# Windowed attention, forward and backward: the order of the DMA transposes on SyncE, the place of one gather, and who copies which rows

## The chip, the cores and the metric

The kernel runs on one core of a Trainium2 chip. A core has five engines, each with its own instruction queue: TensorE (PE: matmuls, with its weight loads as PEld), VectorE (DVE), ScalarE (ACT), GpSimd (POOL) and SyncE (SP), which here only starts transfers. Sixteen DMA engines move the data. The metric is device time in microseconds (us), as the median of several runs; a profiled execution gives a trace of every instruction and every DMA packet.

## What is computed

The input x is an image of 256 × 256 positions with C = 384 channels in bfloat16, cut into 1024 windows of 8 × 8 = 64 tokens. Each window goes through one attention head of width 384 and an output projection. Wanted are the output and the gradients of x, wqkv and wo for a given grad_out.

```python
def _fwd_reference(x, wqkv, wo):
    ...
    qkv = xw @ wqkv
    q, k, v = (qkv[..., :C].copy(), qkv[..., C:2 * C].copy(), qkv[..., 2 * C:].copy())
    scale = C ** (-0.5)
    p = _softmax(jnp.einsum('bqc,bkc->bqk', q, k) * scale, axis=-1)
    o = jnp.einsum('bqk,bkc->bqc', p, v) @ wo
    ...
    _out, _vjp = jax.vjp(_f, x, wqkv, wo)
    _grads = _vjp(grad_out)
```

## The kernel before

**Algebra.** q and k are never formed. With A = scale·Wq·Wkᵀ and B = Wv·Wo, both made once at the start, the scores are x·A·xᵀ and the output is P·(x·B). Per token the kernel forms y (x times A) and z (the output gradient times Bᵀ), both with channels on the partitions, and u = x·B and v = x·Aᵀ with tokens on the partitions. Weight gradients are gathered in two sums, GF_acc, and turned into the gradients of wqkv and wo after the last window.

**Tiles.** Eight windows (a column of 64 rows and 8 columns) are a *quad*: QUAD = 4 tiles of 128 tokens, two windows each. There are 128 quads. For each, x and grad_out are loaded with tokens on the partitions (xq, dq), and both are needed transposed as well (xT, dT); the transposes are done by the DMA engines, started from SP, except for the first quads, which TensorE transposes. Two more DMA transposes per quad follow: `to_tokens` (L174) turns z and y, gathered in zy, into tok (24 blocks of 128 × 128), and `turn` (L244) turns the probabilities and their gradients, stacked in ps, into PS (4 blocks). xT and dT have 12 blocks each.

**Order.** The kernel writes the order of every engine's instructions out by hand (`manual_schedule`); each engine executes its own in the order of the program. The outer loop (L453) runs a step for each i. In step i three quads are in work: a = i+1 gets its projections z and y (`project`, L154), b = i its scores, softmax and u and v (`scores`, `soft`, `uv`), and c = i-1 its attention products and outputs (`attention`, `attend`). The step also loads quad i+3 (`load`, L122: two of the four x tiles from SP, all gradient tiles from POOL; the other two x tiles from ACT, `load_rest`). Ahead of step i, `load_turn` (L134) starts dT and xT of quad i+2.

So SP issues, in each round: dT and xT of quad i+2 (L139), PS of quad i (L246), two x tiles of quad i+3 (L127), tok of quad i+1 (L176). An instruction that has to wait holds up all that stand behind it on the same engine.

**Who uses what.** xT of quad i+2 is read from the y projections of step i+1 on, dT by the z projections of that step. tok and PS of quad i are read by the attention of step i+1. The buffers: xT has 3, dT 2, zy 2, tok 3, PS 2, x 10, dq 6. A z gather of quad i+2 therefore overwrites the zy that tok of quad i was read from, and xT of quad i+2 needs x of quad i+2, loaded in step i-1.

**Copies.** All matmul results go through eight PSUM banks (`ring`), each freed when VectorE or ScalarE has copied it out. The table EV (L388) says who copies: a letter for each tile, D for VectorE, A for ScalarE. "d" is the gradient of x: tile t's copy is of a bank that holds halves of two tiles; the first covers 64 rows, and a fifth copy covers the last 64.

**The gathers.** `gather` (L168) copies z (kind 0) and y (kind 1) out of the interleaved yz into zy, 128 × 1536 values each, on VectorE. The z gather comes ahead of the y projections, the y gather inside the attention of the step: `attention` yields after every tile, and L380 to L384 put the gather behind the first one:

```python
        slots = attention(c) if c is not None else iter(())
        next(slots, None)
        A(gather, 1)
        A(to_tokens)
        for rest in slots:
            pass
```

Of the kernel before, what the change touches and what calls it, by code (L numbers as in the profile page):

```python
# [17 lines left out]
QUAD = 4  # L18
# [4 lines left out]
def kernel(  # L23
# [22 lines left out]
    _, H, W, C = x.shape  # L46
# [27 lines left out]
    def fetch_weights():  # L74
        nc.sync.dma_start(out=w_sb[:, :, columns(2)], in_=w_in[:, :, columns(2)])
        nc.scalar.dma_start(out=wo_sb[:], in_=wo.rearrange("(m p) n -> p m n", p=P))
        for k in (0, 1):
            nc.scalar.dma_start(out=w_sb[:, :, columns(k)], in_=w_in[:, :, columns(k)])

    def warm_up(n):  # L80
        zero = B_sb[:].rearrange("p m c -> p (m c)")[:, 0:4 * P]
        nc.vector.memset(zero, 0.0)
        for i in range(n):
            pt = ring.tile([P, 4 * P], F32, tag="r", name="warm")
            nc.tensor.matmul(pt[:], lhsT=zero[:, 0:P], rhs=zero, start=True, stop=True)
# [25 lines left out]
    def weight_rest():  # L111
        weight_product(B_sb, wT[2], wo_sb, None)
        weight_product(AT_sb, wT[1], wT[0], scale)
# [8 lines left out]
    def load(st, on_act=0):  # L122
        st["xq"] = xq = grp.tile([P, QUAD, C], BF16, tag="xq", name="xq", bufs=2 * GQ + 4)
        st["dq"] = dq = qp.tile([P, QUAD, C], BF16, tag="dq", name="dq", bufs=6)
        for t in range(QUAD):
            if t < QUAD - on_act:
                nc.sync.dma_start(out=xq[:, t, :], in_=windows(x, st, 2 * t))  # L127
            nc.gpsimd.dma_start(out=dq[:, t, :], in_=windows(grad_out, st, 2 * t))  # L128

    def load_rest(st, on_act):  # L130
        for t in range(QUAD - on_act, QUAD):
            nc.scalar.dma_start(out=st["xq"][:, t, :], in_=windows(x, st, 2 * t))

    def load_turn(st):  # L134
        st["xT"] = qp.tile([P, QUAD, CK, P], BF16, tag="xT", name="xT", bufs=3)
        st["dT"] = qp.tile([P, QUAD, CK, P], BF16, tag="dT", name="dT")
        for src, dst, on_pe in (("dq", "dT", G_ON_PE), ("xq", "xT", X_ON_PE)):
            if st["i"] >= on_pe:
                nc.sync.dma_start_transpose(out=st[dst][:].rearrange("p t m k -> p (t m) k"),  # L139
                                            in_=st[src][:].rearrange("p t c -> p (t c)"))  # L140
# [13 lines left out]
    def project(st, kind, mo):  # L154
# [8 lines left out]
        if kind == 0:  # L163
            ENG[EV["z"][mo]](out=yz[:, mo, :, 0:4:3, :], in_=pj[:])  # L164
        else:
            ENG[EV["y"][mo]](out=yz[:, mo, :, 1:3, :], in_=pj[:])  # L166

# [6 lines left out]
    def to_tokens(st):  # L174
        st["tok"] = tok = qp.tile([P, 2, CK, QUAD, P], BF16, tag="tok", name="tok", bufs=3)
        nc.sync.dma_start_transpose(out=tok[:].rearrange("p b m t k -> p (b m t) k"),  # L176
                                    in_=st["zy"][:].rearrange("p b m t s k -> p (b m t s k)"))
# [10 lines left out]
    def over_k(ap, n=P):  # L188
        return ap.unsqueeze(2).broadcast_to([n, QUAD, WT])

    def soft(st, step):
        sd = st["sd"]
        if step == 0:
# [40 lines left out]
    def uv(st, t, part):  # L234
        if t == 0 and part == 0:
            for n in ("uq", "vq"):
                st[n] = qp.tile([P, QUAD, C], BF16, tag=n, name=n)
        wgt, dst, cp = ((B_sb, st["uq"], ENG[EV["u"][t]]), (AT_sb, st["vq"], ENG[EV["v"][t]]))[part]
        pj = ring.tile([P, C], F32, tag="r")
# [16 lines left out]
    def attend(st, t):  # L256
# [5 lines left out]
        def bank(name):  # L262
            return ring.tile([P, C], F32, tag="r", name=name)

        def slot(bank, straight, crossed, start=False, stop=False):
            for h in (LO, HI):
                o = OTHER[h.start]
                products = [(h, bank, straight, {"start": True, "stop": True}),
                            (o, pd[h is LO], crossed, {"start": start, "stop": stop})]
                for o, dst, (lhs, rhs), flags in products if h == LO else products[::-1]:  # L270
                    nc.tensor.matmul(dst[o, :], lhsT=operand(st, lhs, t, h), rhs=operand(st, rhs, t, h), **flags)  # L271

        def keep(name, src, i, rows=slice(0, P)):
            sb = ob.tile([P, C], BF16, tag=name, name=name)
            copies[EV[name][i]](out=sb[rows, :], in_=src[rows, :])  # L275
            return sb[rows, :]
# [4 lines left out]
        slot(pw, ("Pb", "dq"), ("Pb", "z"), start=True)  # L281
        copies[EV["W"][t]](out=st["Wq"][:, t, :], in_=pw[:])  # L282
        pu = bank("pu")
        slot(pu, ("ST", "xq"), ("dS", "y"))
        copies[EV["U"][t]](out=st["Uq"][:, t, :], in_=pu[:])  # L285
        po = bank("po")
# [18 lines left out]
    def gf_rows(sts, f, ma):  # L305
        pw = ring.tile([P, C], F32, tag="r", name="pg")
        n = len(sts) * QUAD
        for i in range(n):
            st, t = sts[i // QUAD], i % QUAD
            product(pw[:], st["xq"][:, t, ma * P:(ma + 1) * P], st["UW"[f] + "q"][:, t, :], i == 0, i == n - 1)  # L310
        gf_add(f, ma, [pw])
# [23 lines left out]
    def attention(st):  # L335
        halves = gf_halves(*fill.pop(0)) if fill else iter(())
        for t in range(QUAD):
            attend(st, t)
            yield
            for k in range(QUAD):  # L340
                next(halves, None)

    def step(c, b, a, ahead):


        def on(st):
            return (lambda f, *r: f(st, *r)) if st is not None else (lambda f, *r: None)
        C_, B, A = on(c), on(b), on(a)
        B(scores)
        B(soft, 0)  # L350
        if b is not None and c is None:
            weight_rest()
        B(uv, 0, 0)
        B(uv, 0, 1)
        B(soft, 1)
        B(uv, 1, 0)
        B(uv, 1, 1)
        B(soft, 2)
        B(soft, 3)
        B(uv, 2, 0)  # L360
        B(uv, 2, 1)
        B(stack)
        B(uv, 3, 0)
        B(uv, 3, 1)
        B(soft, 4)
        for mo in range(CK):
            A(project, 0, mo)
        B(soft, 5)
        B(turn)
        if ahead is not None:  # L370
            load(ahead, ON_ACT)
        A(gather, 0)
        for mo in range(CK):
            A(project, 1, mo)
        if ahead is not None:
            load_rest(ahead, ON_ACT)
        if fill:
            gf_rows(*fill.pop(0))
        slots = attention(c) if c is not None else iter(())
        next(slots, None)  # L380
        A(gather, 1)
        A(to_tokens)
        for rest in slots:
            pass  # L384

    G_ON_PE, X_ON_PE = 4, 1
    ON_ACT = 2
    EV = {"z": "AAA", "y": "AAA", "u": "AAAA", "v": "AAAA", "o": "AAAA", "U": "DDDD", "W": "AAAA", "d": "ADADA"}  # L388
    quads = [(row, col) for row in range(0, H, 2 * WIN * QUAD) for col in range(0, W, WIN)]
    sts = [{"at": q, "i": i} for i, q in enumerate(quads)]  # L390
    n = len(sts)
# [41 lines left out]
    with tc.manual_schedule(engines=MANUAL):  # L433
        fetch_weights()
        warm_up(9)
        load(sts[0])
        make_identity(nc, ident[:])
        load(sts[1])
        load(sts[2])
        load_turn(sts[0])  # L440
        load_turn(sts[1])
        turn_blocks(wT[2], w_sb, 2 * CK)
        weight_product(BT_sb, wo_sb, wT[2], None)
        turn_on_pe(sts[0], "dq", "dT")
        turn_on_pe(sts[0], "xq", "xT")
        turn_blocks(wT[0], w_sb, 0)
        turn_blocks(wT[1], w_sb, CK)
        weight_product(A_sb, wT[0], wT[1], scale)
        nc.vector.memset(GF_acc[:], 0.0)
        held = []  # L450
        last = None
        get = lambda i: sts[i] if 0 <= i < n else None
        for i in range(-1, n + 1):  # L453
            if 0 <= i < n - 2:
                load_turn(sts[i + 2])
            step(get(i - 1), get(i), get(i + 1), get(i + AHEAD) if i >= 0 else None)
            if 0 < i + 2 < G_ON_PE:
                turn_on_pe(sts[i + 2], "dq", "dT")
            if i == 1:
                turn_blocks(woT_sb, wo_sb)  # L460
            if i > 0:
                held.append(sts[i - 1])
                sts[i - 1] = None
            if held and i == n:
                last = gf_final(held)
            elif len(held) == GQ:
                fill.extend((held, f, ma) for f in range(2) for ma in range(CK))
                held = []
        while fill:
            gf_rows(*fill.pop(0))  # L470
        weight_gradients(last)
# [30 lines left out]
```

## Time and profile before

| what | us |
|---|---|
| median of 3 runs | 1970.7 (1964.26 to 1988.57) |
| the profiled execution's own time | 1950.73 |
| its span, first to last instruction | 1948.6 |
| TensorE busy | 1917.4 |
| ScalarE busy | 1591.7 |
| VectorE busy | 1469.0 |
| GpSimd busy | 894.3 |
| one undisturbed step, from the score matmuls to the next step's | 14.67 |
| mean issue on SP: tok, xT, dT, PS | 5.88, 3.04, 2.38, 1.43 |

How to read it: the times of the engines overlap, so they don't add up to the span. SP's instructions start transfers and are not counted as busy; the duration of one is the time until SP has handed the whole transfer over. "To landing" is the time from the start of an issue until its data has arrived. In lists of waits the three numbers are the total, how often, and the longest. In the chain of waits and in timelines the first two numbers are the start and the duration in us, and x is how many instructions are merged. The granted clock is the share of full speed that TensorE was allowed.

### The profile page before, as it was taken

The page shows a single profiled execution, that of the slowest core. Times are in us where ns is not written, and L with a number is a line of the kernel's source. Part 1 is how long each engine was busy: PE and PEld are TensorE (multiplying, and loading weights), DVE is VectorE, ACT ScalarE, POOL GpSimd, SP SyncE. Part 2 cuts the span into 40 slices and gives each one's busy share as a digit, 9 for nine tenths or more (in the row PEclk, how much of TensorE's full clock was granted, in tenths as well). Part 3 has the DMA queues.
Part 4 walks back from the last instruction along what each step waited for, and adds up shares of the span by engine and source line. Part 5 has one row for each costly group of instructions (what it writes and reads, how often), then busy time and mean ns, then how long its engine had stood idle before and what let it go on. Part 6 is the DMA issues. An engine that isn't in the chain of part 4 may idle for free.

```text
span 1948.6 us, 58253 instructions
## 1 busy us (share of the span) xinstructions
PE 1917.4 (98%) x22359; PEld 1145.0 (59%) x22359; DVE 1469.0 (75%) x3241; ACT 1591.7 (82%) x3613; POOL 894.3 (46%) x1670
## 2 busy tenths in 40 slices
PE   9999999999989999999999999999999999999999
PEld 5565565656655566556556556656656655555655
DVE  5777776777767777777777777777777776777776
ACT  7888887888878888888888888888888877887885
POOL 3445454444444445445445444444544444444442
PEclk9999999999999999999999999999999999999999
DMA  9999999999999999999999999999999999999994
GB/s 189 230 229 218 220 225 202 236 221 225 214 198 223 217 227 230 218 231 226 225 228 218 231 215 224 233 215 231 229 221 232 204 219 186 233 222 214 227 210 102
DMA packets 1017623, 423.81 MB, mean 217 GB/s; under 512 B 899584, under 2 KB 992768, under 8 KB 1017344
## 3 DMA queue, kind: packets, MB, share of 16 engines
q1 hardware_dynamic: 899984, 243.25, 77.6%
q0 software_dynamic: 79872, 151.17, 32.7%
q10 hardware_dynamic: 37488, 25.67, 5.5%
q8 instruction: 175, 2.87, 0.6%
q14 instruction: 104, 0.85, 0.2%
HBM read 101.84 MB, written 101.84 MB: 105 GB/s over the span
## 4 chain that ended last, share of the span: by engine, by line
PE 91%; DMA 5%; ACT 2%; DVE 1%; SPq 0%; issue 0%; ACTq 0%
PE pj L150 47%; PE pg L150 13%; PE ph L321 12%; PE sd L150 5%; PE pw L271 5%; PE po L271 4%; DMA xT<-xq 4%; PE pu L271 4%; DMA dT<-dq 1%; PE pd L271 1%; DMA xq<-in_x_dram 0%; ACT yz L164 0%; ACT uq L242 0%; ACT vq L242 0%; ACT yz L166 0%
## 5 line engine op out<-in xcount | busy, mean ns | idle before, releaser
L291 POOL DMA_DIRECT2D out_dram<-o x512 | 273.6, 534 | 779.1 <-ACT o L275 748.1
L150 PEld LDWEIGHTS <-xT 128*128 128x128 bf16 x3072 | 291.9, 98 | 182.3
L282 ACT CAST Wq<-pw 128x384 bf16<-128x384 f32 x512 | 245.0, 479 | 164.3 <-PE pw L271 152.9
L150 PE MATMUL pj<-B_sb,xT 128*128 128x384 bf16 x1536 | 333.4, 326 | 0.0
L150 PE MATMUL pj<-AT_sb,xT 128*128 128x384 bf16 x1536 | 333.3, 326 | 0.0
L128 POOL DMA_DIRECT2D dq<-in_grad_out_dram x512 | 272.6, 543 | 98.3 <-DMA out_dram<-o 43.5
L292 POOL DMA_DIRECT2D out_dram<-d x512 | 278.7, 544 | 74.2 <-DVE d L275 52.6
L285 DVE CAST Uq<-pu 128x384 bf16<-128x384 f32 x512 | 283.1, 553 | 36.6 <-PE pu L271 5.7
L150 PE MATMUL pj<-xT,A_sb 128*128 128x512 bf16 x1152 | 275.0, 385 | 12.9 <-DMA xT<-xq 12.9
L242 ACT CAST uq<-pj 128x384 bf16<-128x384 f32 x512 | 242.5, 474 | 52.2 <-PE pj L150 47.8
L150 PE MATMUL pj<-dT,BT_sb 128*128 128x512 bf16 x1152 | 273.1, 383 | 8.3 <-DMA dT<-dq 8.3
L303 DVE TENSOR_TENSOR GF_acc<-pg,GF_acc 128x384 f32<-128x384 f32 x133 | 74.1, 557 | 242.9 <-PE pg L150 242.9
L242 ACT CAST vq<-pj 128x384 bf16<-128x384 f32 x512 | 246.2, 481 | 2.4
L275 ACT CAST o<-po 128x384 bf16<-128x384 f32 x512 | 247.8, 484 | 0.2 <-PE po L271 0.2
L150 PEld LDWEIGHTS <-xq 128*128 128x128 bf16 x1572 | 154.3, 98 | 116.9 <-issue 3.8
L166 ACT CAST yz<-pj 128x512 bf16<-128x512 f32 x384 | 209.2, 653 | 15.2 <-PE pj L150 14.3
L321 PEld LDWEIGHTS <-xq 64*64 64x64 bf16 x6000 | 187.1, 107 | 52.7
L164 ACT CAST yz<-pj 128x512 bf16<-128x512 f32 x384 | 203.4, 618 | 10.0 <-PE pj L150 9.9
L321 PE MATMUL ph<-Wq,xq 64*64 64x384 bf16 x3984 | 206.3, 322 | 0.0
L150 PEld LDWEIGHTS <-A_sb 128*128 128x128 bf16 x1152 | 113.3, 99 | 154.2 <-DMA xT<-xq 16.6
L150 PEld LDWEIGHTS <-BT_sb 128*128 128x128 bf16 x1152 | 113.3, 98 | 133.2 <-DMA dT<-dq 9.1
L275 ACT CAST d<-pd 64x384 bf16<-64x384 f32 (+1 forms) x384 | 184.1, 479 | 3.1
(86 smaller groups left out, 3369.5 us busy)
## 6 DMA issues: line engine op xcount, KB each, us to landing
dq<-in_grad_out_dram POOLq DMA_DIRECT2D x512, 96.0 KB, 6.4
out_dram<-o POOLq DMA_DIRECT2D x512, 96.0 KB, 4.9
out_dram<-d POOLq DMA_DIRECT2D x384, 96.0 KB, 5.8
xq<-in_x_dram SPq DMA_DIRECT2D x262, 96.0 KB, 4.7
xq<-in_x_dram ACTq DMA_DIRECT2D x250, 96.0 KB, 5.5
out_dram<-d POOLq DMA_DIRECT2D x256, 48.0 KB, 5.6
tok<-zy SPq DMA_TRANSPOSE x128, 11.0
PS<-ps SPq DMA_TRANSPOSE x128, 5.2
```

Of the source, the lines that this page charges most:

```text
L128: nc.gpsimd.dma_start(out=dq[:, t, :], in_=windows(grad_out, st, 2 * t))
L150: nc.tensor.matmul(out, lhsT=lhsT, rhs=rhs, start=start, stop=stop)
L164: ENG[EV["z"][mo]](out=yz[:, mo, :, 0:4:3, :], in_=pj[:])
L166: ENG[EV["y"][mo]](out=yz[:, mo, :, 1:3, :], in_=pj[:])
L242: cp(out=dst[:, t, :], in_=pj[:])
L271: nc.tensor.matmul(dst[o, :], lhsT=operand(st, lhs, t, h), rhs=operand(st, rhs, t, h), **flags)
L275: copies[EV[name][i]](out=sb[rows, :], in_=src[rows, :])
L282: copies[EV["W"][t]](out=st["Wq"][:, t, :], in_=pw[:])
L285: copies[EV["U"][t]](out=st["Uq"][:, t, :], in_=pu[:])
L291: nc.gpsimd.dma_start(out=windows(out_0, st, 2 * t), in_=o)
L292: nc.gpsimd.dma_start(out=windows(out_1, st, first, 2 * t + 1 - first), in_=d)
L321: nc.tensor.matmul(dst[o, :], lhsT=st["xq"][h, t, ma * P + o.start:ma * P + o.stop], rhs=st["UW"[f] + "q"][h, t, :], start=(i == 0), stop= ...
```

## The change

Three things. `to_tokens` leaves the step: it is called in the outer loop, for quad i, ahead of step i and behind `load_turn` of quad i+2, where before it was called for quad i+1 at the end of step i. On SP, tok of a quad so stands behind dT and xT of the quad two further on, and the round is dT, xT, tok, PS, two x tiles. The y gather stands behind the second tile of the attention instead of the first. And "d" is dealt DADAA instead of ADADA: VectorE copies tiles 0 and 2, ScalarE 1, 3 and the last half.

```diff
         slots = attention(c) if c is not None else iter(())
-        next(slots, None)
-        A(gather, 1)
-        A(to_tokens)
+        for t in range(QUAD):
+            if t == 2:
+                A(gather, 1)
+            next(slots, None)
         for rest in slots:
             pass
...
-    EV = {"z": "AAA", "y": "AAA", "u": "AAAA", "v": "AAAA", "o": "AAAA", "U": "DDDD", "W": "AAAA", "d": "ADADA"}
+    EV = {"z": "AAA", "y": "AAA", "u": "AAAA", "v": "AAAA", "o": "AAAA", "U": "DDDD", "W": "AAAA", "d": "DADAA"}
...
             if 0 <= i < n - 2:
                 load_turn(sts[i + 2])
+            if 0 <= i < n:
+                to_tokens(sts[i])
             step(get(i - 1), get(i), get(i + 1), get(i + AHEAD) if i >= 0 else None)
```

## The prediction

> **What bounds the kernel now.** I read the page first, then TensorE's waits, then the chain of waits around a stall, then the timeline of SyncE's queue (SP).
>
> ```profile
> PE 1917.4 (98%) x22359; PEld 1145.0 (59%) x22359; DVE 1469.0 (75%) x3241; ACT 1591.7 (82%) x3613; POOL 894.3 (46%) x1670
> ...
> DMA  9999999999999999999999999999999999999994
> ...
> q1 hardware_dynamic: 899984, 243.25, 77.6%
> ...
> tok<-zy SPq DMA_TRANSPOSE x128, 11.0
> PS<-ps SPq DMA_TRANSPOSE x128, 5.2
> xT<-xq SPq DMA_TRANSPOSE x127, 7.2
> dT<-dq SPq DMA_TRANSPOSE x124, 6.8
> ```
>
> Two resources are full: TensorE, busy for 98% of the span, and the DMA engines, busy in every slice. q1 holds SP's transfers, and its transposes are most of the load. The last four rows give the microseconds from issue to landing.
>
> ```profile
> PE pj L150 <- DMA xT<-xq: 12.9, 6, 4.3
> PE pj L150 <- DMA dT<-dq: 8.3, 2, 4.2
> ```
>
> TensorE waits for little (total, times, longest), and nearly all of it is xT and dT landing late. From one step's first score matmul to the next the trace has 14.67 us in 115 of 127 steps. Three early ones are shorter (12.2 to 12.9), nine are longer: 14.9, 15.7, 16.2, 16.8, 18.6, 18.8, 20.8, 21.6 and 21.9, together 32.9 us over 14.67. That is more than the 21 us of waits, for a slow stretch follows a long one: in the window 573.0 to 577.1, after a wait of 4.33 us, the granted clock is 0.50 and nine projection matmuls take 4.02 us instead of 2.11. In the chain of waits the same place reads:
>
> ```profile
> 540.29 1.95 PE pg L150 x12
> ...
> 543.82 10.04 DMA xT<-xq
> ...
> 559.11 13.92 DMA xT<-xq
> 573.08 4.02 PE pj L150 x9
> ```
>
> SP's timeline in an undisturbed step (start, duration):
>
> ```profile
> 499.47 1.19 SPq L246 DMA_TRANSPOSE PS<-ps  x1
> 500.72 1.22 SPq L127 DMA_DIRECT2D xq<-in_x_dram  x2
> 502.04 6.24 SPq L176 DMA_TRANSPOSE tok<-zy  x1
> 508.51 1.93 SPq L139 DMA_TRANSPOSE dT<-dq  x1
> 510.61 2.96 SPq L139 DMA_TRANSPOSE xT<-xq  x1
> 513.73 1.19 SPq L246 DMA_TRANSPOSE PS<-ps  x1
> 514.97 1.24 SPq L127 DMA_DIRECT2D xq<-in_x_dram  x2
> 516.31 6.34 SPq L176 DMA_TRANSPOSE tok<-zy  x1
> ```
>
> SP issues one after another without a pause, and its round (502.04 to 516.31) is as long as TensorE's step. It can go faster when it is late: after a stall, the round from 1673.25 to 1686.86 took 13.6 us, and the tok issue at 1686.86 took 4.98.
>
> The room, counted from the score matmuls at 502.36: xT lands at 510.61 + 7.2 = 15.5 us and is first used at 21.2 (508.85 in this step, one step of 14.67 later), so it has 5.7 us. dT has 6.3, PS 8.7, tok 14.5 by the same sums. A DMA disturbance of over 5.7 us stops TensorE.
>
> **The change, part by part.** No byte and no matmul is added. (1) tok of quad i goes behind dT and xT of quad i+2. Those two move up by a tok (6.2 us of issue), tok moves back by dT and xT (about 5). Order after, per round: dT, xT, tok, PS, two xq loads. SP is the only queue it is moved past; POOL and ACT issue what they did.
>
> (2) What it adds is a wait. xT of quad i+2 reads the x tile whose second half SP loads just ahead of it. Before, tok's 6.2 us of issue lay between; now only dT's 1.9. The row "xq<-in_x_dram SPq" of the DMA issues gives 4.7 us from issue to landing, so from the first of the two issues to the start of xT it is about 0.65 + 4.7 = 5.35. SP stands still for 5.35 - 1.22 - 1.93 - 0.3 = 1.9 us per round, and behind it wait tok, PS and the next x loads. The round is then a loop: 5.35 + xT + tok + PS + four gaps (0.6).
> - Upper end: mean issue times as now (the tok, xT and PS rows: 5.88, 3.04, 1.43): 16.3 us, 1.6 over the step; over 124 rounds +202, less the 33 of today's stalls which it swallows: +169.
> - Lower end: the shortest issues of these rows (3.96, 1.43, 1.19): 12.5 us, below the step: no cost.
> - Taken: xT starts into a nearly drained queue, so near its short end, 1.8; PS 1.2; tok between its typical 5.98 and the 4.98 of the late rounds. Loop 13.9 to 14.9: on the step, 14.67. Where it is a little over, it slides later until tok is in its faster stretch, as it does now. I take no lost time, but about 1 us of the room.
>
> The Trainium skill, "DMA: Bandwidth & Descriptors", section "Rules for kernel authors", speaks against the change: issue a transfer early and wait on its semaphore late; here the wait comes right behind the issue. The same page, "Anatomy of one DMA", fits 2.0 us plus bytes over 436e3 for GpSimd's queue; for 96 KB that would be an estimated 2.2 us, the wait would shrink to nothing and the forecast would lose its 1 us of room. The row says 4.7 us, on SP's queue under load, and I go by the row.
>
> (3) Room after. With x issued as now, xT starts at about 3.7 us behind the score matmuls, tok at 5.8, PS at 11.8. xT lands at 11 (used 21.2), tok at 5.8 + 11.0 = 16.8 (used 25.2), PS at 17.0 (used 25.3). tok has a second reader: the z gather of quad i+2 overwrites the zy it reads, at 22.9 (510.63 one step on); VectorE would wait there, but has until the GF_acc add at 25.2 before anything of TensorE's depends on it. The narrowest room is about 8 us instead of 5.7; less the 1 of (2), +1.3. Each of eight separate stalls (the 15.7 and 21.9 belong together) gives back at most 1.3: 0.2 + 7 × 1.3 = 9 us. Bounds: 0, if the loop takes all the new room, and 33, if no stall is left.
>
> (4) The y gather goes from behind tile 0 to behind tile 1, from 513.88 to about 515.1, into the place of tile 1's d copy (0.55 us each). SP fetches zy only at 5.8 us of the next step, so it hides under that; it becomes visible if SP ever reaches tok early. (5) Copies: VectorE takes d of tiles 0 and 2, ScalarE of 1 and 3; two and three as before. On ScalarE one more 0.48 us copy stands ahead of the first uq copy, on VectorE one less ahead of the row maximum (504.03). The cover is the eight PSUM banks: TensorE waits for ScalarE's copies 1.2 us in the whole span. If that cover were gone: up to 0.2 us per step, 26 us. I take zero.
>
> **Sum.** The profiled execution took 1950.7 us (span 1948.6 and 2.1 around). 1950.7 - 9 + 0 = 1942. The median of the runs is 20 above that execution; carried over, 1962 against 1970.7, which is no change by the measure of 2% that a measurement of this kernel can tell.
>
> **Rivals.**
> - *The wait on x becomes the bound (slower).* Place: SP ahead of xT. Price: with tok at 5.88, PS at 1.43 and xT between 1.8 and 2.4 (dT's mean issue) the loop is 15.1 to 15.7. At 15.4: 124 × 0.73 = 91, less 33, +58: 2028. It decides from the point where 124 × (L - 14.67) - 33 exceeds 39, L = 15.25. For it: SP has no pause today, so a pause of 1.9 must be made up by shorter issues. Against: the issues are stretched by full DMA engines, and rounds of 13.6 exist.
> - *The whole gain.* The DMA engines lose nothing in the pause, the loop settles as early as now or earlier, room 8 or more, and stalls fall to about 7: -26 in the profiled execution. If the other runs' 20 us are stalls as well, 53 × 26/33 = 42: 1929. For it: all waits of TensorE are xT and dT, the two that are put first. Against: disturbances of one round at 1618 and 309 cost 6 to 9 us, more than any room here.
> - *Nothing comes of it.* tok and PS are late in place of xT: 1971. For it: the DMA engines are full, and the order of transfers adds no capacity.
>
> **How the numbers follow.** Forecast (stalls a little shorter, 1962; own range 1945 to 1985): 0.44. Nothing: 0.12. Slower rival: 0.31, of it 0.05 below +2%. Whole gain: 0.13, of it 0.02 within 2%. So faster by over 2% 0.11, within 2% 0.44 + 0.12 + 0.05 + 0.02 = 0.63, slower 0.26. The range runs from the whole gain, 1929, to a little beyond the slower rival's middle, 2035 (L = 15.45); about 0.18 is left out, most of it above.
>
> **What would show it.** Right: TensorE no longer waits for xT or dT; SP shows a pause of 1 to 2 us ahead of xT, ended by the x load; xT's issue falls to about 2 us; the step stays 14.67 almost everywhere; tok issues start near 6 us behind the score matmuls. Wrong: steps of 15 us or more throughout and a clock row below 9 (the slower rival); waits of TensorE or VectorE for tok or PS (nothing). A wait of TensorE for ScalarE of several tens of us would break part 5.

## The result and the profile after

| | before | changed |
|---|---|---|
| median, us | 1967.48 (1958.56 to 1988.57, 4 runs) | 2091.43 (2087.74 to 2100.25, 4 runs) |
| ratio | | 1.0653, 95% interval 1.0594 to 1.0711 |
| span of the profiled execution | 1948.6 | 2098.4 |

The change costs 6.5%; 1962 was forecast, in a range up to 2035. (A ratio leaves out executions more than 1.5% over the fastest of the same kernel, so it is not the quotient of the medians.) The page of the changed kernel: TensorE is idle more often, the DMA engines are not, and they move less per microsecond (mean 202 GB/s, before 217):

```profile
PE 1967.5 (94%) x22359; PEld 1154.0 (55%) x22359; DVE 1472.4 (70%) x3241; ACT 1583.4 (75%) x3613; POOL 914.5 (44%) x1670
...
DMA  8999999999999999999999999999999999999995
...
DMA packets 1017624, 423.82 MB, mean 202 GB/s; under 512 B 899584, under 2 KB 992768, under 8 KB 1017344
...
PE 43%; DMA 35%; ACT 14%; DVE 4%; issue 3%; SPq 0%; ACTq 0%; DVEq 0%
DMA PS<-ps 17%; DMA tok<-zy 17%; PE pj L150 15%; PE ph L321 11%; PE pg L150 4%; PE pu L271 4%; ACT uq L242 3%; PE pw L271 3%; ACT vq L242 3%; PE po L271 3%; ACT d L275 2%; PE sd L150 2%; ACT o L275 1%; ACT ps L232 1%; ACT ex L205 1%
```

In the chain that ended last (the two lines of shares) 35% now belongs to transfers, and they are PS and tok. Before, 5% belonged to them, and they were xT and dT:

```profile
PE 91%; DMA 5%; ACT 2%; DVE 1%; SPq 0%; issue 0%; ACTq 0%
```

TensorE's waits of the changed kernel say the same (total, times, longest):

```profile
PE pd L271 <- DMA tok<-zy: 90.0, 67, 6.2
PE pu L271 <- DMA PS<-ps: 24.9, 52, 1.5
...
PE pj L150 <- DMA xT<-xq: 1.2, 1, 1.2
```

xT is late once and dT never: what the change set out for, it does. What happened in their place shows in SP's timeline (start, duration):

```profile
900.26 1.30 SPq L246 DMA_TRANSPOSE PS<-ps  x1
901.62 1.23 SPq L127 DMA_DIRECT2D xq<-in_x_dram  x2
903.08 1.50 SPq L139 DMA_TRANSPOSE dT<-dq  x1
906.15 1.49 SPq L139 DMA_TRANSPOSE xT<-xq  x1
907.74 5.84 SPq L176 DMA_TRANSPOSE tok<-zy  x1
913.75 2.23 SPq L246 DMA_TRANSPOSE PS<-ps  x1
916.02 1.22 SPq L127 DMA_DIRECT2D xq<-in_x_dram  x2
917.48 1.91 SPq L139 DMA_TRANSPOSE dT<-dq  x1
921.73 1.43 SPq L139 DMA_TRANSPOSE xT<-xq  x1
```

dT ends at 904.58 and xT starts at 906.15; a round later they are 919.39 and 921.73. Those 1.6 and 2.3 us are the pause ahead of xT, and the list of SP's waits names its end:

```profile
SPq L139 <- DMA xq<-in_x_dram: 201.4, 129, 4.2
```

201.4 us over 124 rounds is 1.62 us per round. Before, the same row was 1.3 us in all:

```profile
SPq L139 <- DMA xq<-in_x_dram: 1.3, 2, 0.6
```

The mean of SP's round, from the durations and gaps in the two traces:

| us per round | before | changed |
|---|---|---|
| tok | 5.88 | 6.81 |
| dT | 2.38 | 2.22 |
| xT | 3.04 | 1.65 |
| PS | 1.43 | 1.77 |
| the four transposes | 12.73 | 12.45 |
| two x loads | 1.35 | 1.32 |
| pause | 0 | 1.62 |
| gaps | 0.7 | 0.7 |
| round | 14.8 | 16.1 |

TensorE's undisturbed step is 14.67 us before and 14.56 now. SP's round before was just on it; now it is 1.5 us over, and SP falls back until TensorE waits for tok and PS. The mean of the steps in the changed trace is 2039.7 / 127 = 16.06 us. Of the 150 us by which the span grew, 100 are TensorE's idle time and 50 its busy time, for the same 22359 matmuls; its mean granted clock fell from 0.994 to 0.985.

### The profile page after: what moved, and what is told of

Same layout as the page of the kernel before. It is cut to its first block, busy times and chain, and to the rows that moved or that the text cites. A ratio compares the mean times of both kernels' runs of the same rounds, so it can differ in the third digit from the quotient of the medians.

```text
span 2098.4 us, 58375 instructions
## 1 busy us (share of the span) xinstructions
PE 1967.5 (94%) x22359; PEld 1154.0 (55%) x22359; DVE 1472.4 (70%) x3241; ACT 1583.4 (75%) x3613; POOL 914.5 (44%) x1670
## 4 chain that ended last, share of the span: by engine, by line
PE 43%; DMA 35%; ACT 14%; DVE 4%; issue 3%; SPq 0%; ACTq 0%; DVEq 0%
DMA PS<-ps 17%; DMA tok<-zy 17%; PE pj L150 15%; PE ph L321 11%; PE pg L150 4%; PE pu L271 4%; ACT uq L242 3%; PE pw L271 3%; ACT vq L242 3%; PE po L271 3%; ACT d L275 2%; PE sd L150 2%; ACT o L275 1%; ACT ps L232 1%; ACT ex L205 1%
## 5 line engine op out<-in xcount | busy, mean ns | idle before, releaser
L172 DVE COPY zy<-yz 128x1536 bf16<-128x1536 bf16 x256 | 142.1, 555 | 360.7 <-DMA tok<-zy 354.5
L292 POOL DMA_DIRECT2D out_dram<-d x512 | 303.2, 592 | 20.4 <-DVE d L275 7.0
L150 PE MATMUL pj<-xT,A_sb 128*128 128x512 bf16 x1152 | 269.5, 379 | 1.2 <-DMA xT<-xq 1.2
L271 PE MATMUL pd<-tok,Pb 64*64 64x384 bf16 x1024 | 177.6, 339 | 91.6 <-DMA tok<-zy 90.0
L321 PE MATMUL ph<-Wq,xq 64*64 64x384 bf16 x3984 | 214.5, 334 | 0.0
L271 PE MATMUL pu<-xq,PS 64*64 64x384 bf16 x1024 | 180.1, 339 | 30.9 <-DMA PS<-ps 24.9
L271 PE MATMUL pw<-dq,Pb 64*64 64x384 bf16 x1024 | 206.8, 339 | 0.6 <-DVE d L275 0.6
```

What stands on the lines that cost most here:

```text
L150: nc.tensor.matmul(out, lhsT=lhsT, rhs=rhs, start=start, stop=stop)
L292: nc.gpsimd.dma_start(out=windows(out_1, st, first, 2 * t + 1 - first), in_=d)
L321: nc.tensor.matmul(dst[o, :], lhsT=st["xq"][h, t, ma * P + o.start:ma * P + o.stop], rhs=st["UW"[f] + "q"][h, t, :], start=(i == 0), stop= ...
```

## The experiments

Theory P says that the pause is the cost. Rival Z says it is the lateness of tok itself, with only two zy buffers; VectorE waits 354.5 us for tok in the changed kernel. Rival D says that tok goes slower beside other traffic, rival C that the gather and the copies cost something. The runs were made in three groups, and the kernel before was timed on the same chip in each: 1956.31 us for the first four runs below, 1954.87 for the third zy buffer in both kernels, the other two parts alone and x on GpSimd, 1949.95 for the rest.

**tok moved alone.** The loop of the changed kernel with the y gather behind the first tile and the copies ADADA.

> The token transpose alone is moved; the y gather stays behind the first tile and the copies stay ADADA. Theory P (the pause: SyncE stands still for x tiles that it has just started to load, 201 us in the changed kernel) and rival Z (tok itself is late, and VectorE and TensorE wait for it) both expect the whole loss, 2075 to 2105. Rival C (the gather's new place and the new deal of copies cost their part) expects at least 20 us less than the changed kernel's 2091.

Measured: 2042.98 us (1969.77 to 2097.55, 4 runs), with a pause of 202 us in all in the trace of a run of 2056.5 us. The median is below the range of P and Z and 48 us below the changed kernel, as C expects; but the runs lie too far apart to decide, and the lowest is inside the spread of the kernel before (1933.04 to 1989.66). That the move alone costs time is likely by this run, not shown. The floor of its steps is 14.67.

**x a quad earlier.**

```diff
-            load(ahead, ON_ACT)
+            load_g(ahead)
+        if ahead_x is not None:
+            load_x(ahead_x, ON_ACT)
...
+                 get(i + AHEAD + 1) if i >= 0 else None)
```

> The changed kernel, with x (its SyncE and its ScalarE tiles) loaded a quad earlier, so that x lies there when its transpose is issued; one more x buffer, paid for by one tok buffer less. The place of tok is that of the changed kernel. Theory P: no pause ahead of xT, steps back near 14.67, 1930 to 1985. Rival Z: tok stays as late, VectorE's wait for tok stays near 350 us, 2060 to 2100. Rival D (tok now runs beside other traffic and is slower by itself, 6.8 us of issue against 5.9): tok's issue stays at 6.5 or more and the time stays over 2020.

Measured: 1953.15 us, ratio to before 0.9971 (0.9905 to 1.0036). The whole loss is gone with tok where the change put it. In its timeline xT follows dT at once, and tok's issue is short again (mean 5.65; here 4.40):

```profile
454.99 1.23 SPq L129 DMA_DIRECT2D xq<-in_x_dram  x2
456.45 2.59 SPq L145 DMA_TRANSPOSE dT<-dq  x1
459.15 2.60 SPq L145 DMA_TRANSPOSE xT<-xq  x1
461.86 4.40 SPq L182 DMA_TRANSPOSE tok<-zy  x1
```

VectorE's wait for tok falls to 68.5 us. P holds; Z and D expected over 2020.

**The pause without the move.** The kernel before, with SP's x loads behind tok instead of ahead of it:

```diff
         A(to_tokens)
+        if ahead is not None:
+            load_x(ahead, ON_ACT)
```

> The kernel before with tok where it was, but SyncE's two x loads moved from ahead of tok to behind it, so right ahead of dT and xT: the same wait for x just issued, without the late tok. Theory P: a pause of about 1.6 us per round ahead of xT, rounds of 15.5 to 16.2, 2040 to 2110. Rival Z: nothing is late that was not, 1960 to 1990.

Measured: 2034.97 us, ratio 1.0408 (1.0314 to 1.0502), a little under P's range and far from Z's. The pause is larger than in the changed kernel: xT starts 2.1 us behind dT's end in the mean (changed 1.7, before 0.2). It costs less, because the four issues sum to 11.50 us here, 1.2 less than before. tok is on time, and TensorE waits for xT and dT instead:

```profile
PE pj L160 <- DMA xT<-xq: 46.9, 51, 2.4
PE pj L160 <- DMA dT<-dq: 28.0, 15, 5.8
```

**x loads ahead of tok.** The changed kernel with `load_x(sts[i + AHEAD], ON_ACT)` in the outer loop, ahead of `to_tokens(sts[i])`.

> The changed kernel with SyncE's two x loads of quad i+3 moved up from behind PS to ahead of tok: the round is dT, xT, two x tiles, tok, PS. tok is as late as in the changed kernel, and some 8 us of issue lie between an x load and its transpose. Theory P: no pause; dT and xT have the most room, the stalls of before shrink, 1925 to 1975. Rival Z: 2060 to 2100. Rival D: over 2020, tok's issue 6.5 or more.

Measured: 1998.09 us, ratio 1.0169 (1.0060 to 1.0279). The pause is gone, and about three quarters of the loss with it by the ratios, but not all: above P's range, below those of Z and D. tok starts 11.8 us behind the score matmuls in the median, with 10% of the rounds under 7.8 and 10% over 15.6; with x a quad earlier the median is 8.2. TensorE waits 42.7 us for tok.

**A third zy buffer** for the changed kernel (`bufs=3` for zy, 2 for tok).

> The changed kernel with three zy buffers and two tok buffers in place of two and three: the z gather of quad i+2 has no transpose of quad i to wait for. Theory P (the pause ahead of xT is the cost): VectorE's wait for tok (354 us) goes away, the pause and the slow rounds stay, 2050 to 2100. Rival Z (the late tok against two zy buffers is the cost): back under 1990.

Measured: 2096.73 us (2061.93 to 2099.99, 4 runs). VectorE's 354.5 us of waiting for tok are gone, and little or nothing is gained: even the lowest run is far over Z's 1990. TensorE waits as long as ever:

```profile
PE pd L271 <- DMA tok<-zy: 85.4, 63, 2.9
PE pu L271 <- DMA PS<-ps: 34.8, 63, 2.1
```

That ends Z (SP does not wait for the second tok buffer: tok starts 0.12 us behind xT's issue), and shows how a large wait of an engine with time to spare reads: as a symptom.

**The same for the x loads ahead of tok.** The kernel of 1998 us with three zy and two tok buffers.

> The kernel with the x loads ahead of tok (no pause, 1998 us, VectorE still waiting 175 us for tok and TensorE 43), with three zy buffers and two tok buffers. If what was left there is the late tok against two zy buffers, VectorE's wait goes away and the time comes down to 1930 to 1965; if it stays near 2000, the rest is tok landing too late for the attention itself, or the DMA engines.

Measured: 2003.79 us (1970.84 to 2014.05, 4 runs), ratio 1.0137 (1.0047 to 1.0228), where 1.0169 was measured with two zy buffers. So it is not the zy buffers either. Without a pause, SP's round is too long in this order because the four issues are: 13.00 us with two zy buffers and 13.18 with three, against 12.45 in the changed kernel. With the x loads (1.4) and the gaps (0.8) that is over 15 us. What makes them longer stays open.

**The other two parts alone.** The gather behind the second tile with tok right behind it, and DADAA.

> The other two parts alone: the y gather behind the second tile, with tok right behind it as before, and the copies DADAA. The three kernels so far that carry these parts have steps of 14.56 us where SyncE does not hold them up, those without have 14.67. If that is their doing: 0.11 x 124 = 14 us less than before, about 1942 where the kernel before has 1956; a small gain that the move of tok hides. If not: the floor of the step stays 14.67 and the time that of before.

Measured: 1949.69 us, ratio 0.9951 (0.9905 to 0.9996), steps with a floor of 14.56. Rival C falls: these parts cost nothing, and are rather a small gain that the pause hides.

**The copies alone.**

> The kernel before with the copies dealt DADAA and nothing else; the floor of the step is what is looked at. If the deal of the copies makes the step of 14.56 us: 14.56 here. If the place of the y gather does: 14.67 (the token transpose moved alone, with the gather behind the first tile and ADADA, had 14.67).

Measured, one execution: 1978.36 us, and neither: nearly every step is 15.09 us. TensorE waits in every step for a bank that VectorE has to copy out:

```profile
PE pu L271 <- DVE Uq L285: 39.9, 123, 0.3
```

With d of tile 0 on VectorE and the y gather still behind tile 0, both stand ahead of tile 1's Uq copy. The deal alone costs; whether the 0.11 us of both parts together comes from the gather alone was not tried.

**x on GpSimd.** The changed kernel with SP's two x loads given to POOL, behind the gradient's.

```diff
-                nc.sync.dma_start(out=xq[:, t, :], in_=windows(x, st, 2 * t))
+                (nc.gpsimd if on_act else nc.sync).dma_start(out=xq[:, t, :], in_=windows(x, st, 2 * t))
```

> The changed kernel with SyncE's two x loads given to GpSimd, behind the gradient loads of the same quad: SyncE has no x load to wait for behind itself and 1.3 us less to issue per round; GpSimd issues two more (1.1 us) out of some 8 us of idle time. No buffer changes. Theory P: no pause, 1925 to 1985. Rival Z, as the place of tok in the round is that of the changed kernel: over 2020.

Measured: 2022.98 us, ratio 1.0313 (1.0231 to 1.0394). P's number is missed, and Z's is met, though TensorE waits only 6.0 us for tok here. SP's pause moved rather than went: the rows of its waits are

```profile
SPq L139 <- DMA dq<-in_grad_out_dram: 144.0, 63, 6.0
SPq L139 <- DMA out_dram<-o: 83.5, 62, 4.8
```

dT now waits for GpSimd's transfers, and the four issues sum to 13.84 us. TensorE's largest wait is for ScalarE, which itself waits for a transfer:

```profile
PE pd L271 <- ACT Wq L282: 68.0, 40, 4.8
ACT Wq L282 <- DMA dT<-dq: 144.0, 33, 8.4
```

As a test between P and Z the run is worth little, since it puts new waits in the place of the old one; what each costs is not separated.

**x loads between tok and PS.** As in the run with the x loads ahead of tok, but with `load_x` behind `to_tokens`. Theory F, named here, says that the transposes go at the pace of full DMA engines; the next experiment tries it.

> The changed kernel with SyncE's x loads between tok and PS: the round is dT, xT, tok, two x tiles, PS, so that the issue of PS (1.2 to 1.8 us) and of dT (2.2) cover the x load in place of dT alone. Theory P with F: the pause falls from 1.6 to 0.4 us or less, and 1.2 x 124 = 149 us with it at most: 1945 to 2000. Rival Z: over 2060.

Measured: 1941.65 us, ratio 0.9992 (0.9944 to 1.0040). Moving two 0.6 us issues ahead of PS takes the whole 6.5% away. The pause is 18.8 us in all, as an x load is now covered by PS (1.48 in the mean) and by a dT that has become longer (2.93 in place of 2.22):

```profile
707.63 4.32 SPq L182 DMA_TRANSPOSE tok<-zy  x1
712.00 1.23 SPq L129 DMA_DIRECT2D xq<-in_x_dram  x2
713.39 1.23 SPq L252 DMA_TRANSPOSE PS<-ps  x1
714.86 3.52 SPq L145 DMA_TRANSPOSE dT<-dq  x1
```

**Fewer stores.** Both kernels with `if t == 0:` ahead of the store of o, so that three of a quad's four tiles of the first output are not written.

> The changed kernel without three of the four output stores of a quad (the first output is left unwritten there), so 96 KB x 3 less to move per round. The question is what the issue time of the transposes is made of: in the kernel before the four take 12.7 us per round, in the changed one 12.5 though xT alone has become 1.4 shorter. Theory F (they go at the pace of full DMA engines, so what one issue saves the next one pays, and a pause adds to the round): the sum falls to 9.5 to 11, the pause is absorbed, steps of 14.56 nearly everywhere, 1905 to 1960. Rival S (SyncE needs that time itself for the blocks it hands over): the sum stays near 12.5 and the time over 2050.

> The kernel before without the same three stores: the base of the comparison. Theory F: the four issues fall to 9.5 to 11 us, SyncE gets pauses ahead of tok (waiting for the y gather), no stall of TensorE is left, 1915 to 1925. Rival S: 12.7 us and some stalls as before, 1935 to 1955.

Measured, one execution each: 1906.55 us for the changed kernel, 1918.14 for the one before. With 0.29 of 3.31 MB less per round, the change is no loss: its steps are 14.57 throughout, and that is the 0.11 us of the other two parts. The pause is still there, 144.5 us in all:

```profile
SPq L139 <- DMA xq<-in_x_dram: 144.5, 115, 3.5
```

But the four issues take 11.1 us in place of 12.45, and 11.1 + 1.3 + 0.7 + 1.2 = 14.3 is inside the step of 14.57. Rival S falls for this kernel: by these two executions, what a pause of this size costs depends on how much the DMA engines have to move. Half of F's number is missed: in the kernel before the four issues stay at 12.37, though nothing waits for them there. So their length is not the DMA load alone, and F is not shown as it stands.

## Why the prediction was wrong

*What failed* is part (2), at the value taken: "xT starts into a nearly drained queue, so near its short end, 1.8; PS 1.2; tok between its typical 5.98 and the 4.98 of the late rounds. Loop 13.9 to 14.9". The pause was seen and sized (1.9 forecast, 1.62 measured), and so was xT (1.8 and 1.65). tok was 6.81 and PS 1.77: a loop of 16.1, close to the upper end of 16.3 that had been worked out and put aside. What xT saved, tok and PS paid. A short issue of xT does not mean a drained queue: its last packets end 2.6 us after its issue, in the median of both traces, so tok still stands behind them. The four issues together took 12.73 us before and 12.45 after, so they made up 0.3 us of the 1.62, and the rest came on top. The upper end also priced it well: 124 × (16.1 - 14.67) - 33 = 144, where the spans differ by 150. That is in part luck: its xT was 1.4 too long, its tok and PS together 1.3 too short. And no rule that the sum of the issues stays follows: with the pause alone they made up 1.2 us.

*"It slides later until tok is in its faster stretch, as it does now"* is wrong with it: tok starts 14.7 us behind the score matmuls in the median, where 5.8 was expected, and its issue is 0.9 us longer than before. The late rounds of the kernel before, 13.6 us, had no pause in them and could not speak for a loop that has one.

*Part (1)* was right: TensorE's 21 us of waits for xT and dT are 1.2. *Part (3)* followed from (2): the room was worked out for x loads at their old place; once SP's round is longer than the step, any room is used up. The z gather's wait that it named came (354.5 us), and was harmless by itself, as it also said.

*Parts (4) and (5)* were taken at zero. Together they give 0.11 us per step (ratio 0.9951, 0.9905 to 0.9996). The cover named for the copies, the eight banks, does not hold for the copies alone: they cost 0.42 us per step, beyond the bound of 0.2. Only the row maximum and the first uq copy had been counted, and not the Uq copy of tile 1, the one TensorE was seen waiting for.

*The rivals.* "The wait on x becomes the bound" was the case, with the place right, at 0.31, and with a loop of 15.1 to 15.7 where 16.1 came. Its "for" line, SP has no pause today, so a pause must be made up by shorter issues, was the better argument: they became shorter by only 0.3 us. Of the signs named for it, long steps came, though not throughout (38 of 127 stayed at 14.6), and the clock row stayed at 9. The waits for tok and PS, named as the sign of "nothing comes of it", came with the loss.

*The pages.* The rule of the Trainium skill that was weighed ("DMA: Bandwidth & Descriptors", "Rules for kernel authors": issue early, wait late) holds here: with x loaded a quad earlier the ratio goes from 1.0653 to 0.9971. The fit for GpSimd's queue (same page, "Anatomy of one DMA") would have the pause vanish, by an estimated 2.2 us per x load; the x load from SP took 4.7 us in both traces, and the pause was 1.62 us.

## What to carry to other kernels

If an in-order queue has no pause in a round that is as long as the bounding engine's step, price a new wait on it in full as the upper bound and take that bound seriously; don't credit it with the shorter issue that follows until the sum of all issues has been shown to fall. Here shorter issues made up 0.3 us of 1.62 in one order and 1.2 of 1.9 in another. When a transfer is moved forward, look at what had been covering the one ahead of it: here tok's issue was the cover of an x load, and putting the load ahead of PS as well restored enough of it. A large wait of an engine with time to spare (VectorE, 354 us) is tested by taking it away, and may be worth nothing.

## What the runs showed of the hardware that was not expected

The issue time of a transpose can move to its neighbours: in four kernels with different orders the four issues of a round sum to 12.45 (changed), 12.45 (x between tok and PS), 12.54 (x a quad earlier) and 12.73 us (before), while xT alone goes from 1.65 to 3.10. But the sum is no constant: it is 11.50 with the pause without the move, 13.00 with x ahead of tok and 13.84 with x on GpSimd, for the same transposes, and what sets it stays open. Nine per cent less to move turned a loss of 6.5% into none, in one execution of each kernel. And the share of time in which the DMA engines are busy does not tell how much more they could move: it reads 9 tenths at 217 GB/s, in the changed kernel at 202, and in the kernel before with fewer stores, in which TensorE never waits for a transpose, at 201.
